# The low parts of w_out's and w3's pieces, subtracted by GpSimd in place of VectorE

## The chip, the cores and the metric

One core of one Trainium2 chip runs the whole program. The metric is the device time of one execution in microseconds; the kernel before takes 864.03 us (median of 3 runs, 861.85 to 864.31).

## What is computed

Attention over 4 batches of 12 heads (448 positions, head size 64, scores squashed by `cap * tanh(s / cap)`), then a gated layer without nonlinearity, then a layer with a softmax-weighted activation and a layer norm:

```python
a = x @ w1                  # x: 1792 x 768, from attention
b = x @ w2
h = a * b @ w3              # 1024 x 1024
x = h @ w_out               # 1024 x 768
h = x @ w_in                # 768 x 1024
# softmax-weighted h, layer norm with g_ln
out = ln @ w_out2           # 1024 x 768
```

The weights arrive in 64-bit floats; everything is computed in 32 bits. To keep precision, most products are split: each operand is written as a high part (rounded to the matmul's 32-bit format, F32R) and a low part (the rest), and three products (high by high, high by low, low by high) are summed.

## The kernel before

**The fold.** `w3 @ w_out @ w_in` does not depend on x, so the kernel multiplies these weights into one 1024 x 1024 matrix while attention runs. Its first stage (line 343) multiplies w_out's pieces by w3's: 4 quarters `fq` of 6 groups `c`, each group 8 blocks `g` of 3 products, 576 matmuls of 256 columns in all. Its second stage (line 361) multiplies the result by w_in.

**The pieces.** Each weight is cut into pieces of 128 x 512 values. `plan64` (line 176) enters one piece in a list with its steps: SyncE loads the piece as pairs of 32-bit words into one of three `ld` buffers; `convert` (lines 167 to 169) puts a 32-bit float together from the two words with three VectorE instructions, into one of two `cv` buffers; `rest` (line 180) then calls `split` (line 172): ScalarE copies the value to the high tile `th` (line 173) and VectorE subtracts `th` from it into the low tile `tl` (line 174). The key of a piece names its weight: `("o", c, i)` for w_out, 12 pieces; `("3", fq, g2)` for w3, 16 pieces; `("i", ...)` for w_in and `("w", ...)` for w1 and w2. The first piece of w_out and those of w3's first quarter come first, then the rest of w_out, then the rest of w3, then w_in. The tiles of w_out appear in the profile as `w_o`, those of w3 as `w`, those of w_in as `w_i` or `w`, those of w1 and w2 as `wt`.

**Attention.** 24 pairs of heads, two steps each. `split_pair` (lines 204 to 216) has VectorE split q, k and v; `scores` (line 228) multiplies q by k; `exps` has ScalarE do tanh and exp (lines 234 and 235); `split_scores` (lines 244 to 249) splits the result on ScalarE and VectorE; `values` multiplies it by v (lines 261 and 265) and sends rows and sums on by DMAs that GpSimd issues (lines 272, 281 and 285). The first two pairs are not split; their products with v (line 261) are plain 32-bit ones and take four times as long. Between the steps, `ahead.step` converts one more piece and `fill` puts in some 4.6 us of the other work, the fold first.

**Order.** The program order above is only a priority. When the program is built, a planner plays its timeline through (`schedule_with_timeline_sim=True`, line 862) and fixes the order in which each engine runs its instructions; on the chip every engine then goes through its queue in that order and waits by semaphores. After attention (about 470 us) come the gated layer (line 560, already started beside attention) and the last two layers (line 681).

GpSimd's own work before is small: the DMAs named above and that of line 424, memsets, and at the end of each row block of the last part one power of a 128 x 1 column (line 739).

Of the kernel before, what the change touches and what calls it, by code (L numbers as in the profile page):

```python
# [14 lines left out]
ALU = mybir.AluOpType  # L15
# [29 lines left out]
def raw(ap):  # L45

    return ap.bitcast(F32)
# [50 lines left out]
def attention_moe_solu(ctx: ExitStack, tc: tile.TileContext, q, k, v, cap, w12, w3t, wo, win, wout2, g_ln, out):  # L98
# [9 lines left out]
    pe, act, dve, pool, sync = nc.tensor, nc.scalar, nc.vector, nc.gpsimd, nc.sync  # L108
# [38 lines left out]
    lands, cvs = {}, {}  # L147

    def landing(i, src, n, kind):
        t = conv.tile([P, 2 * HALF], U32, tag="ld", bufs=LANDS, name=f"ld{i}")  # L150
        lands[i] = t[:, :n].bitcast(kind)
        dst = lands[i]
        if len(src.shape) == 3:
            dst = dst.rearrange("p (a b) -> p a b", a=src.shape[1])
        elif len(src.shape) == 4:
            dst = dst.rearrange("p (a b c) -> p a b c", a=src.shape[1], b=src.shape[2])
            for g in range(src.shape[1]):
                sync.dma_start(out=dst[:, g], in_=src[:, g])
            return
        sync.dma_start(out=dst, in_=src)  # L160

    def convert(i, n):

        d = lands.pop(i).rearrange("p (n w) -> p n w", w=2)
        lo, hi = d[:, :, 0], d[:, :, 1]
        x = conv.tile([P, HALF], U32, tag="cv", bufs=2, name=f"cv{i}")[:, :n]
        dve.tensor_scalar(x, hi, 5, 2, ALU.logical_shift_left, ALU.logical_shift_right)  # L167
        dve.scalar_tensor_tensor(x, hi, 0xC0000000, x, ALU.bitwise_and, ALU.bitwise_or)  # L168
        dve.scalar_tensor_tensor(x, lo, 29, x, ALU.logical_shift_right, ALU.bitwise_or)  # L169
        cvs[i] = x.bitcast(F32)  # L170

    def split(th, tl, x):
        act.copy(th, x)  # L173
        dve.tensor_tensor(tl, x, raw(th), ALU.subtract)  # L174

    def plan64(key, src, n, dst, gate=None, there=None):

        i = len(ahead.items)

        def rest():  # L180
            th, tl = dst()
            split(th, tl, cvs.pop(i))
        ahead.add(key, lambda: landing(i, src.bitcast(U32), 2 * n, U32), lambda: convert(i, n), rest, gate, there)


# [140 lines left out]
    def load34(f, nh):  # L326
        i = f"34_{f}_{nh}"
        landing(i, w34_dr[f].rearrange("p c k -> p (c k)"), NC * P, F32)
        t = ev_p.tile([P, 2, NC * P], F32R, tag="w34", bufs=2, name=f"w34_{f}_{nh}")
        split(t[:, 0], t[:, 1], lands.pop(i))  # L330
        return t.rearrange("p a (c k) -> p a c k", c=NC)
# [80 lines left out]
    def plan_x(b):  # L412
        for part in range(NPAIR // 2):
            if (b, part) == (B - 1, NPAIR // 2 - 1):

                plan_again(NF + 2)
            i = len(ahead.items)
            pairs = slice(2 * part, 2 * part + 2)

            def load(i=i, pairs=pairs):  # L420
                rb[i] = conv.tile([P, 2, S], F32, tag="rb", name=f"rb{i}")
                for j in range(2):
                    row = r_dr[b].rearrange("(n j) s -> j n s", j=2)[j:j + 1, pairs]
                    pool.dma_start(out=rb[i][j * D:(j + 1) * D], in_=row.to_broadcast([D, 2, S]))

            def first(i=i, part=part):

                for c in (2 * part, 2 * part + 1):
                    xs[b, c] = place_x(b, c)
                one = raw(xs[b, 2 * part + 1][:, 0, :1])  # L430
                pool.memset(one, 1.0)
                dve.scalar_tensor_tensor(xr[b, part], xr[b, part], one, rb.pop(i), ALU.mult, ALU.mult)

            def rest(part=part):
                x = xr.pop((b, part))
                for i in range(2):
                    split(xs[b, 2 * part + i][:, 0], xs[b, 2 * part + i][:, 1], x[:, i])
            ahead.add(("x", b, part), load, first, rest, None, lambda part=part: free_x(b, part))
# [430 lines left out]
```

## Time and profile before

| | us |
|---|---|
| median of 3 runs | 864.03 |
| span of the profiled execution | 863.1 |
| PE busy | 836.1 (97%) |
| VectorE (DVE) busy | 615.3 (71%) |
| ScalarE (ACT) busy | 500.4 (58%) |
| GpSimd (POOL) busy | 75.6 (9%) |

The busy shares are averages over the whole span, and the stages differ: the change lies in the first 107 us. In the profile, PE is TensorE's matmul, PEld its weight load, a line such as L174 is a line of the kernel, and a row `tl<-x,th` names what an instruction writes and reads. The granted clock stands as a share of 2.4 GHz.

### The profile page before, as it was taken

How to read it: one execution, taken by the hardware profiler on the slowest of the kernel's cores; microseconds unless marked ns; L12 is line 12 of the kernel's file. 1: busy time of each engine (PE TensorE's matmuls, PEld its weight loads, DVE VectorE, ACT ScalarE, POOL GpSimd, SP SyncE). 2: the span in 40 equal slices, each digit the busy share in tenths (PEclk: the TensorE clock that was granted, in tenths of full speed). 3: DMA queues.
4: the chain of work that ended last, by engine and by line, in shares of the span. 5: the costliest groups of instructions: out<-in, count | busy, mean ns of one | idle time of the engine just before them, and what ended most of it. 6: DMA issues, size and time to landing. Idle time of an engine off the chain costs nothing.

```text
span 863.1 us, 12409 instructions
## 1 busy us (share of the span) xinstructions
PE 836.1 (97%) x4420; PEld 688.9 (80%) x4420; DVE 615.3 (71%) x1090; ACT 500.4 (58%) x745; POOL 75.6 (9%) x147
## 2 busy tenths in 40 slices
PE   6999999999999999999999999999999999889998
PEld 4678988667677777777667999998788888789998
DVE  7989987987965589778865453444788786975452
ACT  4779477898967687676755202202555556653331
POOL 1011001101111111010101100000000000100000
PEclk7999999999999999999999999999999999999999
DMA  7877876787964376477758699893533224672211
GB/s 252 264 208 220 238 212 184 229 270 195 281 188 144 89 227 226 170 223 247 252 181 291 207 361 402 318 343 118 171 122 98 98 98 152 203 256 104 104 62 74
DMA packets 91550, 174.28 MB, mean 202 GB/s; under 512 B 9696, under 2 KB 58080, under 8 KB 89440
## 3 DMA queue, kind: packets, MB, share of 16 engines
q1 hardware_dynamic: 86496, 162.30, 57.3%
q0 software_dynamic: 4992, 11.19, 5.2%
q8 instruction: 35, 0.57, 0.3%
q14 instruction: 27, 0.22, 0.1%
HBM read 117.18 MB, written 50.68 MB: 194 GB/s over the span
## 4 chain that ended last, share of the span: by engine, by line
PE 76%; DMA 10%; DVE 8%; ACT 3%; issue 3%; SPq 0%; POOL 0%; DVEq 0%; POOLq 0%; ACTq 0%
PE ab L560 20%; PE u L681 13%; PE f L343 8%; PE o L265 8%; PE f L361 7%; PE sc L228 6%; PE v L681 6%; DMA wg_dr<-cv 4%; PE y L681 3%; PE o L261 2%; PE tp L748 1%; DVE cv L168 1%; DVE cv L169 1%; DMA rb<-r_dr 1%; DMA r_dr<-inv 1%
## 5 line engine op out<-in xcount | busy, mean ns | idle before, releaser
L560 PE MATMUL ab<-xs,wt 128*128 128x448 f32 x1152 | 247.1, 369 | 0.6 <-ACT a L564 0.6
L560 PEld LDWEIGHTS ab<-xs,wt 128*128 128x128 f32 x1152 | 215.1, 189 | 28.1 <-issue 8.9
L234 ACT ACTIVATE sc<-sc,qscale 128x896 f32<-128x896 f32 x96 | 93.5, 978 | 31.3 <-PE sc L228 31.3
L235 ACT ACTIVATE p<-sc,capt 128x896 f32<-128x896 f32 x96 | 96.9, 1015 | 1.7 <-PE o L261 0.6
L265 PE MATMUL o<-hi,v 128*66 128x448 f32 x352 | 96.7, 366 | 1.2 <-DVE hi L249 1.2
L681 PE MATMUL u<-ws,a 128*128 128x512 f32 x336 | 83.1, 398 | 3.3 <-ACT u L685 2.1
L247 DVE TENSOR_TENSOR lo<-p,hi 128x896 fp32r<-128x896 f32 x66 | 71.5, 1084 | 17.2 <-ACT hi L244 16.9
L343 PEld LDWEIGHTS f<-w,w_o 128*128 128x128 f32 x576 | 72.9, 191 | 8.6 <-issue 3.3
L343 PE MATMUL f<-w,w_o 128*128 128x256 f32 x576 | 78.5, 288 | 0.0
L681 PEld LDWEIGHTS u<-ws,a 128*128 128x128 f32 x336 | 63.8, 191 | 18.0 <-ACT u L685 2.6
L361 PE MATMUL f<-w_i,w 128*128 128x512 f32 x288 | 74.6, 400 | 0.6 <-DVE w L174 0.6
L681 PE MATMUL u<-wg,c 128*128 128x384 f32 x336 | 65.5, 340 | 3.4 <-ACT wg L173 1.3
L361 PEld LDWEIGHTS f<-w_i,w 128*128 128x128 f32 x288 | 52.4, 188 | 18.0 <-issue 5.7
L265 PEld LDWEIGHTS o<-hi,v 128*66 128x66 f32 x352 | 47.2, 136 | 24.3 <-DVE hi L249 2.4
L244 ACT CAST hi<-p 128x896 fp32r<-128x896 f32 x66 | 62.6, 950 | 0.1
L681 PEld LDWEIGHTS u<-wg,c 128*128 128x128 f32 x336 | 58.2, 188 | 4.5 <-DVE wg L174 2.8
L167 DVE TENSOR_SCALAR cv<-ld 128x512 uint32<-128x512 uint32 (+1 forms) x80 | 32.7, 410 | 30.0 <-DMA wg_dr<-cv 18.5
L228 PE MATMUL sc<-qh,kh 64*128 64x448 f32 x192 | 43.8, 452 | 10.4 <-ACT p L235 10.4
L168 DVE SCALAR_TENSOR_TENSOR cv<-ld,cv 128x512 uint32<-128x512 uint32 (+1 forms) x80 | 52.5, 660 | 0.9
L169 DVE SCALAR_TENSOR_TENSOR cv<-ld,cv 128x512 uint32<-128x512 uint32 (+1 forms) x80 | 52.5, 659 | 0.6
L564 ACT COPY a<-ab 128x448 f32<-128x448 f32 x32 | 17.1, 534 | 59.8 <-PE ab L560 59.8
L272 POOL DMA_DIRECT2D xr<-x x48 | 26.0, 544 | 287.1 <-ACT x L271 286.7
(124 smaller groups left out, 1255.2 us busy)
## 6 DMA issues: line engine op xcount, KB each, us to landing
ld<-in_w SPq DMA_DIRECT2D x24, 512.0 KB, 4.9
w_dr<-wt SPq DMA_DIRECT2D x8, 1536.0 KB, 7.3
wt<-w_dr SPq DMA_DIRECT2D x8, 1536.0 KB, 9.4
ld<-in_w3t SPq DMA_DIRECT2D x16, 512.0 KB, 4.2
ab_dr<-abs SPq DMA_DIRECT2D x32, 224.0 KB, 4.4
ldab<-ab_dr SPq DMA_DIRECT2D x14, 512.0 KB, 4.0
c_dr<-e SPq DMA_DIRECT2D x14, 512.0 KB, 2.8
ldc<-c_dr SPq DMA_DIRECT2D x14, 512.0 KB, 4.3
```

Source lines behind the costliest of these rows:

```text
L168: dve.scalar_tensor_tensor(x, hi, 0xC0000000, x, ALU.bitwise_and, ALU.bitwise_or)
L169: dve.scalar_tensor_tensor(x, lo, 29, x, ALU.logical_shift_right, ALU.bitwise_or)
L228: pe.matmul(sc[:, j, :S], kk[rows, c * P:(c + 1) * P], qq[rows, :], start=(m == 0), stop=(m == 2))
L234: act.activation(sc[:, :, :S], sc[:, :, :S], AF.Tanh, scale=qscale)
L235: act.activation(p, sc[:, :, :S], AF.Exp, scale=capt)
L244: (act.copy if c < 3 else dve.tensor_copy)(hi, p)
L247: dve.tensor_tensor(lo, p, raw(hi), ALU.subtract)
L265: pe.matmul(o[:VW, :S], vs[:, a, j, c], t[:, j], start=(c == 0 and i == 0), stop=(c == 3 and i == 1))
L343: pe.matmul(f[:, :QW], lw[:, a], rw[:, e], start=(g == 0 and m == 0), stop=(g == NF - 1 and m == 2))
L361: pe.matmul(f, w34[:, a, c, :], rw[:, e], start=(c == 0 and m == 0), stop=(c == NC - 1 and m == 2))
L560: pe.matmul(pp[f, b, i][:, :S], w[:, u], xs[b, c][:, e], start=(c == 0 and m == 0), stop=(c == NC - 1 and m == 2))
L681: pe.matmul(bank, a[m][:, x, k * P:(k + 1) * P], wb[m][:, e, k, :], start=(first and k == 0 and i == 0), stop=(k == NF // 2 - 1 and i == 2 ...
```

## The change

`split` gets a parameter for the engine that subtracts, and `plan64` passes GpSimd (`pool`) for pieces whose key begins with "o" or "3". All other calls of `split` keep VectorE.

```diff
-    def split(th, tl, x):
+    def split(th, tl, x, low=dve):
         act.copy(th, x)
-        dve.tensor_tensor(tl, x, raw(th), ALU.subtract)
+        low.tensor_tensor(tl, x, raw(th), ALU.subtract)
 ...
         def rest():
             th, tl = dst()
-            split(th, tl, cvs.pop(i))
+            split(th, tl, cvs.pop(i), pool if key[0] in ("o", "3") else dve)
```

## Rows read from the trace of the kernel before

**Rows 1.** Windows: start:end, length, busy (x instructions) per engine, PEclk, DMA share, GB/s
```profile
10.00:62.00 52.00, 45.58 (x239) 28.95 (x239) 48.51 (x94) 38.23 (x53) 5.16 (x9) 0.90 0.80 238
62.00:82.00 20.00, 20.00 (x132) 15.02 (x130) 19.88 (x34) 18.45 (x26) 1.95 (x3) 1.00 0.79 230
82.00:113.00 31.00, 31.00 (x249) 29.80 (x248) 27.97 (x51) 14.52 (x27) 2.13 (x4) 1.00 0.79 228
```

**Rows 2.** Instructions of line 174: duration min/median/max ns, first and last start, forms
```profile
L174 DVE TENSOR_TENSOR w<-cv,w x16: 673/684/692, 19.0 to 105.6; 128x512 fp32r<-128x512 f32 x16
...
L174 DVE TENSOR_TENSOR w_o<-cv,w_o x12: 625/685/690, 11.7 to 60.2; 128x512 fp32r<-128x512 f32 x12
```

**Rows 3.** VectorE in order of time: start, us, instruction [idle before it]
```profile
21.33 0.69 DVE L168 SCALAR_TENSOR_TENSOR cv<-ld,cv 128x512 uint32<-128x512 uint32 x1
21.94 0.68 DVE L174 TENSOR_TENSOR w<-cv,w 128x512 fp32r<-128x512 f32 x1
22.54 0.68 DVE L169 SCALAR_TENSOR_TENSOR cv<-ld,cv 128x512 uint32<-128x512 uint32 x1
```

**Rows 4.** TensorE and its weight loads, 0 to 125 us: what they waited for, us, times, longest
```profile
PE sc L228 <- ACT p L235: 6.6, 1, 6.6
...
PEld f L343 <- DVE cv L169: 1.2, 3, 0.7
...
PEld f L343 <- DVE cv L167: 0.9, 2, 0.7
```

**Rows 5.** GpSimd by line: count | busy us, mean ns
```profile
L621 POOL MEMSET v<- 128x1056 f32 x2 | 1.9, 978 | 0.3 <-POOLq L862 0.3
...
L622 POOL MEMSET v<- 128x8 f32 x2 | 0.1, 112 | 0.0
```

**Rows 6.** Line 739, GpSimd's only two-operand instruction: duration min/median/max ns
```profile
L739 POOL TENSOR_TENSOR st<-st,neghalf x14: 547/549/2335, 637.0 to 759.1; 128x1 f32<-128x1 f32 x14
```

**Rows 7.** GpSimd, then VectorE, in order of time around the longest of them
```profile
738.66 2.33 POOL L739 TENSOR_TENSOR st<-st,neghalf 128x1 f32<-128x1 f32 x1 [4.37 <-DVE st L738]
...
738.42 0.96 DVE L174 TENSOR_TENSOR wg<-ldwg,wg 128x768 fp32r<-128x768 f32 x1
739.28 1.30 DVE L174 TENSOR_TENSOR c<-cs,c 128x512 fp32r<-128x512 f32 x2
740.49 0.70 DVE L704 TENSOR_TENSOR h<-v,u 128x512 f32<-128x512 f32 x1
```

**Rows 8.** GpSimd, then VectorE, around a shorter one
```profile
658.98 0.99 POOL L739 TENSOR_TENSOR st<-st,neghalf 128x1 f32<-128x1 f32 x1 [19.46 <-DVE st L736]
...
658.88 0.68 DVE L174 TENSOR_TENSOR a<-s,a 128x512 fp32r<-128x512 f32 x1
```

**Rows 9.** VectorE: two pieces' subtractions, for the second and the last w_out group
```profile
31.86 0.69 DVE L174 TENSOR_TENSOR w_o<-cv,w_o 128x512 fp32r<-128x512 f32 x1
...
60.21 0.69 DVE L174 TENSOR_TENSOR w_o<-cv,w_o 128x512 fp32r<-128x512 f32 x1
```

**Rows 10.** TensorE in order of time: first products with these two pieces, and quarter 2's start
```profile
33.81 1.93 PE L343 MATMUL f<-w,w_o 128*128 128x256 f32 x12
...
62.25 0.50 PE L343 MATMUL f<-w,w_o 128*128 128x256 f32 x2
...
95.39 2.42 PE L343 MATMUL f<-w,w_o 128*128 128x256 f32 x19
```

**Rows 11.** VectorE: the subtraction for w3's piece (2, 0)
```profile
82.27 0.68 DVE L174 TENSOR_TENSOR w<-cv,w 128x512 fp32r<-128x512 f32 x1
```

**Rows 12.** VectorE at the start, in order of time
```profile
11.11 0.69 DVE L168 SCALAR_TENSOR_TENSOR cv<-ld,cv 128x512 uint32<-128x512 uint32 x1
11.72 0.68 DVE L174 TENSOR_TENSOR w_o<-cv,w_o 128x512 fp32r<-128x512 f32 x1
12.32 0.69 DVE L169 SCALAR_TENSOR_TENSOR cv<-ld,cv 128x512 uint32<-128x512 uint32 x1
```

**Rows 13.** ScalarE at the start, in order of time
```profile
10.77 0.62 ACT L173 CAST w_o<-cv 128x512 fp32r<-128x512 f32 x1 [7.00 <-DVE cv L169]
13.04 0.62 ACT L173 CAST w_o<-cv 128x512 fp32r<-128x512 f32 x1 [1.65 <-DVE cv L169]
13.57 1.87 ACT L234 ACTIVATE sc<-sc,qscale 128x896 f32<-128x896 f32 x2
```

**Rows 14.** TensorE at the start, in order of time
```profile
9.48 0.37 PE L228 MATMUL sc<-ql,kh 64*128 64x448 f32 x2
16.42 0.74 PE L228 MATMUL sc<-qh,kh 64*128 64x448 f32 x2 [6.57 <-ACT p L235]
```

**Rows 15.** TensorE in order of time after two waits near the end of attention
```profile
451.73 0.48 PE L228 MATMUL sc<-qh,kh 64*128 64x448 f32 x2 [1.16 <-ACT p L235]
...
454.89 0.60 PE L228 MATMUL sc<-qh,kh 64*128 64x448 f32 x2 [1.47 <-ACT p L235]
```

**Rows 16.** Windows, as in rows 1, of the stretch behind these waits
```profile
456.00:459.10 3.10, 3.10 (x11) 2.66 (x10) 3.06 (x7) 2.60 (x5) 1.61 (x3) 0.60 0.73 211
```

## The prediction

> **What bounds the kernel now.** I read the busy shares by stage first, because the change lies in one stage: all 28 subtractions run between 11.7 and 106.3 us [rows 2]. There the reader is to see two engines full at once. VectorE is busy 48.5 of 52 us between 10 and 62, 19.9 of 20 up to 82, 28.0 of 31 up to 113; TensorE is busy without a gap in the last two [rows 1]. GpSimd is busy 5.2, 2.0 and 2.1 us. Next the waits: TensorE's only long one is 6.6 us for ScalarE's first exp, and for VectorE's conversions its weight loads waited 1.2 and 0.9 us [rows 4]. So in this stage TensorE sets the time, and VectorE runs just ahead of it. How far ahead is read by setting a piece's subtraction beside the first product that needs it, counting line 343's matmuls (24 to a group, 12 to a w_out piece). The piece for the second group is done at 32.55 and used at 33.81, 1.26 us later; the last w_out piece is done at 60.90 and used at 62.25, 1.35 us later [rows 9, 10]. Later the lead is wide: w3's piece (2, 0) is done at 82.95 and used at 95.39 [rows 10, 11].
>
> **What the change removes.** 28 instructions of 684 ns [rows 2]. Back to back they overlap a little: one starts at 21.94, the next at 22.54, so each costs VectorE 0.60 us of its queue [rows 3]. That is 28 x 0.60 = 16.8 us. Nearly none of it is on the path: TensorE waits for VectorE only about 2 us in this stage [rows 4]. One of them is on it, at the start: the second piece's conversion, which ScalarE's second cast waits for, stands behind a subtraction (11.72 to 12.32), and the first tanh stands behind that cast, and TensorE behind the tanh [rows 12 to 14]. Without it the chain is 0.6 us shorter: -0.6.
>
> **What it adds: the subtraction on GpSimd.** No such instruction is in the trace. Its fixed cost is bounded by the nearest two-operand row, 0.55 us for one column [rows 6]. Per column, a memset takes (978 - 112) / 1048 = 0.83 ns [rows 5], so one pass over 512 columns is 0.42 us. If both operands come at once it is 0.55 + 0.42 = 0.97 us, one after the other 0.55 + 0.85 = 1.40. I take 1.2, the middle, with both ends for the range; 0.53 (a memset of that size) is the extreme below. The Trainium skill (GPSIMD Engine Reference, 3.1) gives 4497 ns for a two-operand add of 2048 columns; a quarter is an estimate of 1.12 us, which would make the sum below some 1.6 us smaller; no run here shows it.
>
> **What it adds: the two engines in each other's way.** Line 739 takes 0.55 us when VectorE leaves it alone. Once it takes 2.33: it starts at 738.66, while VectorE runs three subtractions with both operands in SBUF back to back until 740.58, and it ends at 740.99, while VectorE is on an instruction that reads PSUM. Another ends 0.41 us after the single such subtraction beside it, at 659.97 [rows 7, 8]. So a GpSimd instruction that reads stands still while VectorE reads two operands from SBUF. The other direction, VectorE standing still while GpSimd reads 512 columns, is shown by no row, since line 739 reads one column; its price lies between 0 and the whole 1.2 us. I take the whole, because what holds one reader off completely is not likely to let the other through. The Trainium skill (SBUF — State Buffer, "Who interferes with whom") says just this: the read side is shared and locked for a whole instruction, and whoever comes second waits. The trace agrees for GpSimd waiting, with the 2.33 us; for VectorE waiting no run yet speaks.
>
> **The new wait.** The `cv` buffers are two, and a buffer is free only when both cast and subtraction have read it. So the conversion two pieces on (line 167) now waits for GpSimd, and behind it in VectorE's queue stand the next pair's q, k and v and the low parts of the scores, for which TensorE waits next. On GpSimd a subtraction that waits for its cast holds up the DMAs of lines 272, 281, 285 and 424. They feed the gated layer, behind 140 us, and are covered; the cover ends with the sums' DMA of line 281, for which VectorE's reciprocal waits in order.
>
> **The sum.** If neither engine reads while the other does, each piece takes 1.2 - 0.6 = 0.6 us more of the shared time. Up to 62 us there are 16 pieces (12 of w_out, 4 of w3): 16 x 0.6 = 9.6. VectorE was idle 52 - 48.5 = 3.5 us there [rows 1], and the last w_out piece has 1.35 us in hand: TensorE is late by 9.6 - 3.5 - 1.35 = 4.8. Up to 82 us 4 more pieces add 2.4 less 0.1 idle: 7.1 in all. The last 8 add 4.8, less 3.0 idle, and the lead of 12 us covers them: nothing. TensorE late in several short stops also loses clock: behind two stops of 1.16 and 1.47 us the granted clock is 0.60 of 2.4 GHz for 3.1 us [rows 15, 16], a loss of 3.1 x 0.4 = 1.2 us; I count one such spell. TensorE is full behind this stage, so nothing is made up later. Sum: 7.1 + 1.2 - 0.6 = +7.7. The profiled execution's span is 863.1, and 0.9 lies between it and the median of the runs, 864.0. 864.0 + 7.7 = 871.7, say **871.5**. With 0.97 us for a subtraction the terms are 16 x 0.37 - 4.85 = 1.1 and 4 x 0.37 = 1.5, less 0.6: 866. With 1.40 they are 16 x 0.8 - 4.85 = 8.0 and 3.2, two spells of low clock 2.4, less 0.6: 877. The new order that the planner makes is unknown and may move all this by 2 or 3 us.
>
> **Rivals.** *Side by side:* VectorE isn't held by GpSimd's reads. Then a piece is done 1.2 - 0.68 = 0.5 us later than now, less the time it stood in VectorE's queue, and the leads of 1.26 and 1.35 us cover that. What is left is the 0.6 at the start: 863.4, between 862 and 865. For it speaks that no VectorE row is stretched beside line 739; against it, that line 739 reads hardly anything.
>
> *Faster:* VectorE's 16.8 us come free and the planner uses them at the start. Place: the first tanh waits until 13.57 for the second cast, though the scores are there at 9.85 and the first cast ends at 11.39 [rows 13, 14]. With the tanh ahead of that cast TensorE starts 13.57 - 11.39 = 2.2 us sooner, and with it go the waits for conversions, 1 to 2 us: 864.0 - 3.7 = 860.3, between 859 and 861.4. It decides if GpSimd holds VectorE for less than the 0.60 us saved, since otherwise the queue is no shorter. Against it: the tanh's place in the queue is not what the change touches.
>
> *Held twice:* the lock as in my forecast, but GpSimd also loses each race, as in the 2.33 us row, and each handing over costs the 0.41 us that line 739 needs after VectorE lets go [rows 8]. 20 pieces x 0.41 = 8.2 on top: 879.7, between 877 and 886. For it: VectorE hardly has a gap between 62 and 82 us (19.9 of 20). Against it: some instructions there (casts, line 167) read one operand.
>
> **How the numbers follow.** Forecast (866 to 877): 0.47. Held twice: 0.16. Side by side: 0.22. Faster: 0.15. The range leaves out most of *faster* (0.13) and the upper part of *held twice* (0.07): 861.5 to 880. About 0.3%, 2.6 us, is what a measurement of this kernel can tell from no change. Faster by more, below 861.4: 0.15. Within, up to 866.6: 0.22 and a sliver of the forecast, 0.24. Slower: 0.61.
>
> **What would show it.** Right, if the profile after has 28 GpSimd rows of line 174 whose median is above 1 us and some far longer; if VectorE's lines 168, 169 and 205 are stretched or idle beside them; if TensorE shows waits in lines 343 and 228 between 16 and 82 us that add up to some 5 to 8 us; and if the stages behind 113 us are as long as before. Wrong, if VectorE's durations stay as they are and TensorE has no new waits (side by side), if TensorE's first wait is shorter by more than 2 us (faster), or if the loss sits behind 140 us, which I did not cost.

## The result

The change makes the kernel slower: 875.32 us median (874.81 to 876.12) against 864.1 us, a ratio of 1.0136 with an interval of 1.0109 to 1.0163. That is +11.2 us; 871.5 had been forecast, +7.5. The profiled execution's span is 873.0 us, 9.9 more than before.

### The profile after

The same three windows as in [rows 1], of the changed kernel:

```profile
10.00:62.00 52.00, 40.91 (x216) 26.18 (x217) 48.98 (x67) 31.06 (x45) 25.46 (x19) 0.93 0.76 229
62.00:82.00 20.00, 17.10 (x104) 12.34 (x102) 19.22 (x28) 12.80 (x18) 11.06 (x11) 0.95 0.70 204
82.00:113.00 31.00, 29.25 (x212) 25.09 (x212) 28.31 (x41) 18.15 (x30) 12.72 (x10) 0.97 0.71 202
```

VectorE is as full as before (49.0 of 52 us, 19.2 of 20, 28.3 of 31), but runs 67, 28 and 41 instructions in place of 94, 34 and 51; 16, 4 and 8 of the missing ones are the subtractions, the others come later. TensorE stands 11.1 us in the first window (6.4 before), 2.9 in the second and 1.8 in the third (none before), and its granted clock, 1.00 in the last two before, is 0.95 and 0.97 of 2.4 GHz there.

The subtractions, as in [rows 2]:

```profile
L174 POOL TENSOR_TENSOR w<-cv,w x16: 1275/1504/2296, 17.0 to 107.5; 128x512 fp32r<-128x512 f32 x16
...
L174 POOL TENSOR_TENSOR w_o<-cv,w_o x12: 1283/1478/1739, 10.2 to 59.6; 128x512 fp32r<-128x512 f32 x12
```

They take about 1.5 us on GpSimd, where VectorE took 0.68. What they do to VectorE is seen beside single ones. VectorE, in order of time:

```profile
38.30 1.66 DVE L169 SCALAR_TENSOR_TENSOR cv<-ld,cv 128x512 uint32<-128x512 uint32 x1
...
44.12 1.78 DVE L205 TENSOR_TENSOR kl<-kd,kh 128x512 fp32r<-128x512 f32 x1
...
76.71 3.58 DVE L249 TENSOR_TENSOR hi<-p,hi 64x896 fp32r<-64x896 f32 x1
```

GpSimd at the same times:

```profile
37.93 1.48 POOL L174 TENSOR_TENSOR w_o<-cv,w_o 128x512 fp32r<-128x512 f32 x1 [2.47 <-ACT w_o L173]
...
43.76 1.60 POOL L174 TENSOR_TENSOR w_o<-cv,w_o 128x512 fp32r<-128x512 f32 x1 [1.29 <-ACT w_o L173]
...
76.81 2.52 POOL L174 TENSOR_TENSOR w<-cv,w 128x512 fp32r<-128x512 f32 x2
```

Line 169 takes 1.66 us in place of 0.69, line 205 1.78 in place of 0.69, line 249, beside two subtractions, 3.58 in place of 1.09. In the whole profile VectorE is busy 624.4 us, 9.1 more than before, with 28 instructions less. These stood for 16.8 us of its queue, so the others are stretched by 25.9 us, 0.93 a piece. On top come its new waits for GpSimd (waits of VectorE, 0 to 115 us):

```profile
DVE cv L167 <- POOL w L174: 2.4, 2, 1.2
DVE cv L167 <- POOL w_o L174: 2.3, 2, 1.2
```

Together 30.6 us, 1.09 for each of the 28 pieces, against 0.60 saved: VectorE's queue is 13.8 us longer. Where TensorE feels it (waits of its matmuls, from the view of the whole span; those shown all lie before 113 us):

```profile
PE f L343 <- POOL w L174: 2.7, 3, 1.4
PE f L343 <- ACT w_o L173: 2.1, 3, 1.2
...
PE f L343 <- POOL w_o L174: 1.7, 2, 1.2
...
PE f L343 <- ACT e L347: 1.1, 2, 0.8
PE f L343 <- ACT w L173: 1.1, 2, 0.9
```

Before, the matmuls of line 343 had none of these waits. Five of them, 4.4 us, end with a subtraction of GpSimd itself, so that its length, 1.5 us in place of 0.68, has a part in them beside VectorE's longer queue; no run here separates the two. How late the fold is shows in line 343's first and last start (the two times behind the durations). First before, then after:

```profile
L343 PE MATMUL f<-w,w_o x576: 274/283/629, 23.3 to 147.1; 128*128 128x256 f32 x192
```

```profile
L343 PE MATMUL f<-w,w_o x576: 274/283/632, 19.1 to 158.8; 128*128 128x256 f32 x192
```

The fold's first stage ends 11.7 us later. The last product of the gated layer (line 560) is 10.8 us later (607.7 against 596.9), that of line 681 9.9 (868.8 against 858.9). So most of the loss stays, and 1.8 us of it are made up behind this stage in these two executions; the kernel before had there the spell of low clock of [rows 16], and between 458 and 470 us of the changed kernel the granted clock is 1.00.

### The profile page after: what moved, and what is told of

Same layout as the page of the kernel before. It is cut to its first block, busy times and chain, and to the rows that moved or that the text cites. A ratio compares the mean times of both kernels' runs of the same rounds, so it can differ in the third digit from the quotient of the medians.

```text
span 873.0 us, 12429 instructions
## 1 busy us (share of the span) xinstructions
PE 837.3 (96%) x4420; PEld 688.3 (79%) x4420; DVE 624.4 (72%) x1062; ACT 500.5 (57%) x745; POOL 117.7 (13%) x175
## 4 chain that ended last, share of the span: by engine, by line
PE 66%; DVE 14%; DMA 11%; issue 5%; ACT 3%; POOL 1%; SPq 0%; DVEq 0%; ACTq 0%; POOLq 0%
PE ab L560 19%; PE u L681 13%; PE f L361 7%; PE o L265 7%; PE v L681 6%; PE sc L228 5%; PE y L681 4%; DMA wg_dr<-cv 4%; PE f L343 3%; DVE cv L168 2%; DVE cv L167 2%; DVE cv L169 2%; PE tp L748 1%; DMA inv<-x 1%; DMA wt<-w_dr 1%
## 5 line engine op out<-in xcount | busy, mean ns | idle before, releaser
L167 DVE TENSOR_SCALAR cv<-ld 128x512 uint32<-128x512 uint32 (+1 forms) x80 | 36.8, 462 | 33.1 <-DMA wg_dr<-cv 15.0
L169 DVE SCALAR_TENSOR_TENSOR cv<-ld,cv 128x512 uint32<-128x512 uint32 (+1 forms) x80 | 59.6, 748 | 1.0
L168 DVE SCALAR_TENSOR_TENSOR cv<-ld,cv 128x512 uint32<-128x512 uint32 (+1 forms) x80 | 54.3, 682 | 1.0
```

## The experiments

Theory 1 is the forecast's: GpSimd and VectorE exclude each other, VectorE's queue grows, and TensorE runs too close behind it. Theory 2: they run side by side, and the loss comes from low parts that are done later and from the planner's other order. Theory 3: the new wait on the two `cv` buffers is what costs.

Each run below is set beside runs of the kernel before that were taken with it (medians 862.9 to 863.1 us), and its ratio is to those.

**The disputed cost by itself.** Two runs of kernels that leave out the whole computation and hold only stretches of the disputed instructions, kept apart by copies of ScalarE. Of the second (the name of a stretch, how many instructions VectorE and GpSimd run in it, and which; `two` is the subtraction, `bank` one with an operand in PSUM):

```diff
+    phase("pool", 0, 5, None, two(pool))
+    phase("dve", 10, 0, two(dve), None)
+    phase("both", 16, 5, two(dve), two(pool))
+    phase("bank", 16, 5, bank, two(pool))
+    phase("castalone", 10, 0, cast, None)
+    phase("cast", 24, 5, cast, two(pool))
+    phase("shift", 24, 5, shift, two(pool))
+    phase("write", 16, 12, two(dve), write)
```

> The whole computation is left out; only the disputed cost runs, in stretches that are kept apart by copies of ScalarE: five subtractions of 128x512 on GpSimd alone; ten on VectorE alone; then five on GpSimd beside a row of VectorE instructions that read two operands from SBUF, one from SBUF and one from PSUM, that cast, that shift words (as line 167 does); and, last, VectorE subtractions beside GpSimd memsets that hardly read. Theory 1, the engines exclude each other: alone about 1.3 us on GpSimd (the shortest in the changed kernel is 1.28) and 0.60 us from start to start on VectorE; beside each other 16 x 0.60 + 5 x 1.3 = 16 us for the stretch with two SBUF operands, with VectorE rows stretched from 0.69 to over 1.5 us or GpSimd rows to several us; the casts likewise (8 to 9 us become 14); the stretch with PSUM and the one with memsets as if each engine were alone (9.6 us for VectorE). Theory 2, they run side by side and the loss comes from later low parts and another order: 9.6 us in every stretch, and no row longer than when alone.

> The disputed cost by itself again (the whole computation is left out), since in the first such run the word shifts ran beside the GpSimd subtractions that should have run alone, and the memsets ahead of everything. Expected now, if a GpSimd subtraction stops VectorE for 1.08 us whenever VectorE reads two operands from SBUF or casts or shifts at the faster pace: alone 1.23 to 1.27 us on GpSimd (as beside the PSUM reads); 16 VectorE subtractions beside five of GpSimd 15 us; 24 casts beside five 13.5 us against 24 x 0.34 = 8.2; 24 shifts beside five 13.5 us; 16 subtractions beside memsets, which only write, 9.7 us. If only reading two operands matters, casts and shifts are not stopped: 8.2 us.

The second run, VectorE: start, length of the whole stretch, what ran.

```profile
12.82 6.11 DVE L173 TENSOR_TENSOR d_dve<-src_dve,other 128x512 fp32r<-128x512 f32 x10 [11.29 <-ACT src_dve L155]
19.40 15.05 DVE L173 TENSOR_TENSOR d_both<-src_both,other 128x512 fp32r<-128x512 f32 x16 [0.47 <-ACT src_both L154]
34.92 9.65 DVE L176 TENSOR_TENSOR d_bank<-acc,src_bank 128x512 fp32r<-128x512 f32 x16 [0.47 <-ACT src_bank L154]
45.05 3.44 DVE L179 CAST d_castalone<-src_castalone 128x512 fp32r<-128x512 f32 x10 [0.47 <-ACT src_castalone L154]
48.96 13.46 DVE L179 CAST d_cast<-src_cast 128x512 fp32r<-128x512 f32 x24 [0.47 <-ACT src_cast L154]
64.06 12.41 DVE L183 TENSOR_SCALAR d_shift<-words 128x512 uint32<-128x512 uint32 x24 [1.64 <-ACT words L160]
76.95 9.72 DVE L173 TENSOR_TENSOR d_write<-src_write,other 128x512 fp32r<-128x512 f32 x16 [0.47 <-ACT src_write L154]
```

GpSimd in the same run:

```profile
6.21 6.14 POOL L173 TENSOR_TENSOR p_pool<-src_pool,other 128x512 fp32r<-128x512 f32 x5 [5.77 <-ACT src_pool L155]
19.45 8.44 POOL L173 TENSOR_TENSOR p_both<-src_both,other 128x512 fp32r<-128x512 f32 x5 [7.09 <-ACT src_both L154]
34.97 6.17 POOL L173 TENSOR_TENSOR p_bank<-src_bank,other 128x512 fp32r<-128x512 f32 x5 [7.08 <-ACT src_bank L154]
...
77.62 5.71 POOL L186 MEMSET p_write<- 128x512 f32 x12 [7.81 <-ACT p_write L163]
```

Alone a subtraction takes 6.14 / 5 = 1.23 us on GpSimd. Sixteen VectorE subtractions, 9.7 us alone (0.60 each), take 15.05 beside five of GpSimd: 5.4 / 5 = 1.07 us of standstill for each. Twenty-four casts, 24 x 0.34 = 8.2 alone, take 13.46: 1.06 each. The shifts were not measured alone; at the 0.34 us of a cast they would be 8.2, and 4.2 were added, while one of the five subtractions was all but over before they began: by this estimate again about 1.05. With one operand in PSUM nothing is added on either engine, and memsets don't touch the subtractions (9.72). So theory 1's lock holds, with its limits: VectorE stands while GpSimd reads, if it reads two operands from SBUF or casts or shifts; theory 2's *side by side* does not. The rival *held twice*, with 0.41 us on top for each handing over, falls too: 15.05 us are less than the two engines' times one after the other (9.7 + 6.14). The Trainium skill (SBUF — State Buffer, "Who interferes with whom") has this rule, the fast casts included; the trace agrees, with a standstill of 1.07 us for a GpSimd instruction of 1.23. In the first run the shifts had run ahead, beside the subtractions meant to be alone; its other stretches gave the same times (15.05, 9.66, 13.47).

**GpSimd writes instead of reading.** Of the low parts only the first column is subtracted, the rest is zeros:

```diff
-        low.tensor_tensor(tl, x, raw(th), ALU.subtract)
+        if low is pool:
+            pool.tensor_tensor(tl[:, :1], x[:, :1], raw(th)[:, :1], ALU.subtract)
+            pool.memset(raw(tl)[:, 1:], 0.0)
+            pool.memset(raw(tl)[:, 1:], 0.0)
+        else:
+            dve.tensor_tensor(tl, x, raw(th), ALU.subtract)
```

> As the changed kernel, but GpSimd subtracts one column only and then writes zeros twice over the low part (511 columns): of the 28 low parts only the first column is computed. It is busy about as long for a piece (0.55 + 2 x 0.53 = 1.6 us against 1.5 us in the changed kernel), waits for the same casts, frees the same buffers a little earlier, but hardly reads. Theory 1 (the engines exclude each other while GpSimd reads): VectorE's rows have their lengths of before, and the time is 863 to 866 us. Theory 2 (the low part is late because GpSimd takes 1.5 us, and the planner's order is another): 871 to 876 us, as the changed kernel.

865.16 us, ratio 1.0034 (1.0010 to 1.0058). With GpSimd about as busy (115.2 us in all against 117.7), three quarters of the loss are gone, which is for theory 1. But the memsets did not wait for the casts: 18 of w_out's 24 had run by 15.3 us, the other six between 39.2 and 42.4, and w_out's later low parts waited for no more than the one column. This run alone doesn't rule out that late low parts have a share. Not all rows of VectorE have their old lengths, either. By form, xcount | busy us, mean ns:

```profile
L168 DVE SCALAR_TENSOR_TENSOR cv<-ld,cv 128x512 uint32<-128x512 uint32 x64 | 43.6, 686 | 0.8
L169 DVE SCALAR_TENSOR_TENSOR cv<-ld,cv 128x512 uint32<-128x512 uint32 x64 | 43.5, 685 | 0.8
L167 DVE TENSOR_SCALAR cv<-ld 128x512 uint32<-128x512 uint32 x64 | 31.2, 490 | 25.4 <-DMA ld<-in_w 10.6 <-DMA wg_dr<-cv 6.9 <-DMA ld<-in_w3t 3.5
```

The changed kernel, the same view:

```profile
L169 DVE SCALAR_TENSOR_TENSOR cv<-ld,cv 128x512 uint32<-128x512 uint32 x64 | 50.8, 798 | 0.8
L168 DVE SCALAR_TENSOR_TENSOR cv<-ld,cv 128x512 uint32<-128x512 uint32 x64 | 45.5, 716 | 0.8
L167 DVE TENSOR_SCALAR cv<-ld 128x512 uint32<-128x512 uint32 x64 | 31.2, 488 | 21.3 <-DMA ld<-in_w 10.5 <-DMA wg_dr<-cv 5.3 <-POOL w L174 2.4
```

The two-operand lines 168 and 169 are back at 686 and 685 ns (687 and 686 before), but the shift of line 167 stays at 490 (423 before): a memset holds the fast one-operand instructions too, as a single copy at the end of this document shows.

**The same time on VectorE, without GpSimd.** Each of the 28 subtractions is made twice:

```diff
-        low.tensor_tensor(tl, x, raw(th), ALU.subtract)
+        dve.tensor_tensor(tl, x, raw(th), ALU.subtract)
+        if low is pool:
+            dve.tensor_tensor(tl, x, raw(th), ALU.subtract)
```

> GpSimd isn't used; VectorE makes each of the 28 subtractions twice. That lengthens VectorE's queue by 0.60 us a piece, about what the exclusion costs by theory 1 (1.28 on GpSimd less 0.60 saved = 0.68). Theory 1: 28 x 0.60 = 16.8 us more on VectorE have about the effect of the change, 871 to 877 us. Theory 2: VectorE's length isn't what counts, 863 to 866 us.

872.97 us, ratio 1.0134 (1.0088 to 1.0180): 16.8 us more for VectorE cost what the change costs. So a longer queue of VectorE is enough, without GpSimd. The planner's order is rather different here (w3's last piece is subtracted at 154 us), and the second subtraction starts 0.7 to 2.9 us behind the first, so the low parts are later too: this is no exact twin, and it doesn't tell a long queue from late low parts.

**VectorE's time for nothing.** Only one column of the 28 low parts is subtracted, on VectorE; GpSimd's memset fills the rest and waits for nothing:

```diff
-        low.tensor_tensor(tl, x, raw(th), ALU.subtract)
+        if low is pool:
+            dve.tensor_tensor(tl[:, :1], x[:, :1], raw(th)[:, :1], ALU.subtract)
+            pool.memset(raw(tl)[:, 1:], 0.0)
+        else:
+            dve.tensor_tensor(tl, x, raw(th), ALU.subtract)
```

> What VectorE's 16.8 us are worth if nothing is paid for them: VectorE subtracts one column only of the 28 low parts (0.1 us or so in place of 0.60), and GpSimd writes zeros over the rest, without reading and without waiting for a cast; the low parts but for a column are left out. If TensorE alone sets the time of this stage, as I read the profile before, the gain is the start's 0.6 us and the 2 us of waits for conversions: 861 to 864 us. If VectorE sets it together with TensorE, a good part of 28 x 0.5 = 14 us is gained: 850 to 858 us.

864.37 us, ratio 1.0022 (0.9993 to 1.0050). VectorE is busy 606.4 us, 8.9 less than before, and nothing is gained: more VectorE time lengthens this stage, less doesn't shorten it. That fits TensorE setting the time, and the rival *faster* finds nothing for it. It doesn't show that no order could gain, since TensorE has new waits here, for the one-column subtractions (line 175 of this kernel; its line 347 is line 343 before):

```profile
PE f L347 <- DVE w_o L175: 2.8, 2, 1.9
```

**Which pieces cost.** The condition for GpSimd is cut to w_out's 12 pieces, to w3's last 8, to the other 20, and to the first two:

```diff
-            split(th, tl, cvs.pop(i), pool if key[0] in ("o", "3") else dve)
+            split(th, tl, cvs.pop(i), pool if key[0] == "o" else dve)
 ...
+            split(th, tl, cvs.pop(i), pool if key[0] == "3" and key[1] >= 2 else dve)
 ...
+            split(th, tl, cvs.pop(i), pool if key[0] == "o" or key[0] == "3" and key[1] < 2 else dve)
 ...
+            split(th, tl, cvs.pop(i), pool if key[:2] == ("o", 0) else dve)
```

> Only the 12 pieces of w_out go to GpSimd. Their subtractions lie before 62 us, where TensorE is 1.3 us behind VectorE. Theory 1: 12 x 0.68 = 8.2 us more on the shared side, less 3.5 us that VectorE was idle and 1.35 in hand: +3.3, less 0.7 at the start: 866 to 868 us.

867.8 us, ratio 1.0040 (1.0007 to 1.0072): +3.5 us by the ratio, as expected.

> Only the 8 pieces of w3's last two quarters go to GpSimd; their products have a lead of 2.6 to 17 us. Theory 1 as I used it in the prediction (the lead covers them): 863.5 to 865 us. Theory 1 with attention (what VectorE does late for them is not the fold's but the next pairs' q, k, v and scores, which have no lead): 866 to 870 us, since TensorE's lateness in the changed kernel grows by 5.7 us between 80 and 110 us.

865.85 us, ratio 1.0038 (1.0007 to 1.0068): +3.3 us by the ratio. The interval reaches from 0.6 to 5.9, so its lower end is near the forecast's nothing. In the profiled execution TensorE stands once up to 125 us, apart from the start, and a copy of line 347 ends it. ScalarE, then TensorE:

```profile
108.17 0.62 ACT L173 CAST w_i<-cv 128x512 fp32r<-128x512 f32 x1 [2.14 <-DVE cv L169]
108.69 0.64 ACT L347 COPY e<-f 128x256 f32<-128x256 f32 x2
```

```profile
109.11 2.30 PE L343 MATMUL f<-w,w_o 128*128 128x256 f32 x17 [1.44 <-ACT e L347]
```

> The other 20 pieces go to GpSimd, w_out's 12 and w3's first two quarters. Theory 1 as in the prediction: the whole loss is here, 873 to 876 us. Theory 1 with attention: the loss is that of the changed kernel at 80 us, 6.2 us: 869 to 871 us.

871.26 us, ratio 1.0093 (1.0061 to 1.0125): +8.0 us, less than the whole. With the last eight's 3.3 it adds up to 11.3, about the change's 11.2 to 11.7, though both intervals are wide. Between 82 and 113 us TensorE stands 0.1 us here, in place of the changed kernel's 1.8. The lateness quoted in these expectations (6.2 us at 80, 11.9 at 110) is my count: the products done up to then in each trace, times the time of one in a full stretch (0.20 us for 448 columns, 0.41 for an unsplit one of line 261, which is twice as long and not four times, 0.12 for line 343, 0.10 for a score).

> Only the first two pieces of w_out go to GpSimd. They stand ahead of ScalarE's first tanh while TensorE has nothing to do, so the exclusion costs nothing there and the chain is shorter by the one subtraction: TensorE's first wait 5.9 in place of 6.6 us, 0.6 to 0.8 us less in all: 863 to 863.5 us, within what can be measured.

863.04 us, ratio 1.0010 (0.9975 to 1.0044): no difference. TensorE's first wait was 5.0 us there; but it was 5.1 in the run with the last eight pieces, where the first two are VectorE's as before, so this is no sign of the change.

**A third buffer.** For the 28 pieces every third `cv` tile comes from another pool:

```diff
-        x = conv.tile([P, HALF], U32, tag="cv", bufs=2, name=f"cv{i}")[:, :n]
+        third = i < 28 and i % 3 == 2
+        x = (ev_p if third else conv).tile([P, HALF], U32, tag="cv3" if third else "cv", bufs=1 if third else 2, name=f"cv{i}")[:, :n]
```

> As the changed kernel, with a third cv buffer for the 28 pieces, so that line 167 needn't wait for GpSimd's subtraction of two pieces back (4.7 us of waits in four places in the changed kernel). Theory 1: the shared read side is as full as before, the waits move elsewhere: 873 to 876 us. Theory 3, the new wait on the cv buffers is a large part of the loss: 4 to 5 us less, 870 to 871 us.

879.74 us, ratio 1.0204 (1.0163 to 1.0245): 4 us slower than the change, where theory 3 wanted 4 to 5 less and theory 1 about the same. Of the waits of line 167 for GpSimd one of 1.2 us is left. The windows show why it is slower still, again as in [rows 1]:

```profile
10.00:62.00 52.00, 39.71 (x206) 27.67 (x206) 49.98 (x68) 26.17 (x39) 31.29 (x20) 0.84 0.73 227
62.00:82.00 20.00, 17.89 (x69) 12.77 (x70) 19.24 (x24) 9.57 (x15) 10.53 (x7) 0.66 0.74 226
82.00:113.00 31.00, 31.00 (x231) 26.77 (x230) 27.16 (x40) 22.74 (x34) 11.23 (x14) 1.00 0.65 188
```

TensorE stands 14.4 us in the three windows, against 15.7 in the changed kernel, so nearly all of its standing is there without these waits; theory 3 is not the main cause. How much the waits cost in the changed kernel's order stays open, since the granted clock differs: it is 0.84 and 0.66 of 2.4 GHz in the first two windows. TensorE stood, among others, 3.0 us for a copy of line 347's, and worked slowly behind it. The planner had put the queues in another order; which part of the 4 us is the order's and which the clock's, I did not separate.

## Why the prediction was right, and where it was off

*The bound.* Right as far as the runs go. TensorE had no slack to give [rows 1, 4], and VectorE's time counts only upward in them: twice the subtractions cost 1.3%, and one column in place of them gained nothing.

*The subtraction's price on GpSimd.* Taken at 1.2 us, the middle between one and two passes at the memset's pace [rows 5, 6]; alone it is 1.23. That it fell in the middle had no reason in the forecast. Beside VectorE it is 1.5, since it waits its turn too.

*The lock.* Taken as whole, from line 739's 2.33 us [rows 7, 8], for the direction that no row showed. Right: 1.07 us of standstill by itself; in the kernel 0.93 of stretched rows, 1.09 with the waits for `cv` buffers. The forecast counted 1.2.

*The sum up to 82 us.* Forecast 7.1 for 20 pieces, 7.7 with clock and start. Those 20 alone cost 8.0 (5.3 to 10.8). The closeness is in part luck, since two errors offset each other. The standstill is 1.07 - 0.60 = 0.47 us a piece and not 0.6, which is 20 x 0.13 = 2.6 less; but the 3.5 us that VectorE was idle up to 62 us, which the sum took off, were not used up: 52 - 48.98 = 3.0 of them are still there in the changed kernel.

*The last eight pieces.* This step failed: "the lead of 12 us covers them: nothing". They alone cost 3.3 us (0.6 to 5.9), about what the changed kernel loses beyond the other 20. The lead was 12 us for the first of them only, 2.6 for the fourth; it did suffice for line 343's products [rows 10, 11], none of which waits for them in the third window. But VectorE's queue and ScalarE's also carry attention and the groups' copies, which have no such lead. One chain of the changed kernel shows it. VectorE, ScalarE, then TensorE:

```profile
103.51 1.50 DVE L167 TENSOR_SCALAR cv<-ld 128x512 uint32<-128x512 uint32 x1 [1.18 <-POOL w L174]
```

```profile
106.76 0.62 ACT L173 CAST w<-cv 128x512 fp32r<-128x512 f32 x1 [3.42 <-DVE cv L169]
107.29 0.36 ACT L347 COPY e<-f 128x256 f32<-128x256 f32 x1
```

```profile
107.70 0.50 PE L343 MATMUL f<-w,w_o 128*128 128x256 f32 x2 [0.78 <-ACT e L347]
```

The shift waits 1.18 us for GpSimd to free a `cv` buffer; ScalarE waits 3.42 us for the conversion that follows; the copy that empties a finished group's PSUM tile stands behind that cast, and TensorE waits 0.78 us for it. The run with the last eight alone has the same end, a copy of line 347 behind a late cast, without a wait for a buffer: there line 169 is stretched (1.67 us in place of 0.69). The new wait had been named in the forecast with what is queued behind it on VectorE, but not with the second queue behind that, ScalarE's. The planner's order has a part in it: before, ScalarE's copy stood ahead of the cast, as here:

```profile
101.56 0.37 ACT L347 COPY e<-f 128x256 f32<-128x256 f32 x1 [1.86 <-PE f L343]
101.83 0.63 ACT L173 CAST w<-cv 128x512 fp32r<-128x512 f32 x1
```

*The clock.* One spell of 1.2 us was counted. Between 81 and 85 us of the changed kernel, behind the stop of 1.4 us and one of 0.75 for line 249, the window reads:

```profile
81.00:85.00 4.00, 3.44 (x16) 1.68 (x16) 3.96 (x6) 2.49 (x6) 1.69 (x1) 0.68 0.57 163
```

4 x 0.32 = 1.3 us: the size was right.

*The start.* Forecast -0.6, found -0.8 (TensorE's first products after the wait begin at 15.61 in place of 16.42 [rows 14]), but not for the reason given: this agreement is luck. With the subtraction gone from between, VectorE needed longer, not shorter, for the two first conversions: 4.61 us (7.58 to 12.19) against 4.15 (8.86 to 13.01), since the last of them stood 0.94 us for GpSimd:

```profile
10.56 1.63 DVE L169 SCALAR_TENSOR_TENSOR cv<-ld,cv 128x512 uint32<-128x512 uint32 x1
```

The first piece's conversion had begun 1.28 us earlier, because VectorE had not stood for the load of v as in the kernel before:

```profile
7.69 0.43 DVE L211 COPY vf<-vd 128x512 f32<-128x512 f32 x1 [1.82 <-DMA vd<-in_v]
```

The run with the last eight pieces doesn't have this wait either, and with both first subtractions on VectorE TensorE starts sooner still:

```profile
15.35 0.74 PE L228 MATMUL sc<-qh,kh 64*128 64x448 f32 x2 [5.07 <-ACT p L235]
```

So nothing shows a gain at the start by the change.

*What is placed.* The extra standstill of TensorE in the three windows is 4.7 + 2.9 + 1.8 = 9.3 us, by the unrounded times; low clock in the last two adds 20 x 0.05 + 31 x 0.03 = 1.9. About 1.0 is regained at the start, where TensorE works through 3.1 us at a granted clock of 0.50 (15.6 to 18.7), before through 5.2 (16.4 to 21.6). That is 10.2 of the 11.7 us at the fold's end. The rest is about what a stop costs beyond the idle time, by an estimate: idle time counts from the end of a product, 0.28 us behind its start in line 343, where in a full stretch the next starts after 0.12 (19 in 2.42 us [rows 10]); for 14 new stops that is 14 x 0.16 = 2.2. The 0.2 to 0.3% that the two runs with memsets lie above the kernel before are within or just above what can be told, and I can't say whether the order or the memsets make them.

## What to carry to other kernels

Before an elementwise step goes to GpSimd, ask what VectorE does meanwhile: if it reads two operands from SBUF, or casts, GpSimd's read stopped it here for 1.07 us of 1.23, to save 0.60. Relief of an engine that is full is worth only what the engine that sets the time waits for it, here about nothing, while a longer queue can cost nearly its whole length, here 11.2 us for 13.8. And a lead that is measured for one consumer covers only that one: follow a new wait through the second and third in-order queue behind it.

## What the runs showed of the hardware

In a row of VectorE subtractions, GpSimd and VectorE took turns: five GpSimd subtractions took 8.44 us, 1.69 each, about 1.07 + 0.60. Line 739's one-column read had waited through three instructions instead [rows 7]. And a memset, which reads nothing, leaves two-operand subtractions alone (9.72 us for 16) but holds a VectorE copy, as in the run with memsets: a copy of 512 columns, 0.42 us otherwise, took 1.32 beside two, which took 0.98 together. VectorE, then GpSimd:

```profile
14.23 1.32 DVE L216 COPY vf<-vd 128x512 f32<-128x512 f32 x1
```

```profile
14.30 0.98 POOL L177 MEMSET w_o<- 128x511 f32 x2
```
